# Two decode attention blocks, rewritten from heads in pairs to heads in fours, with one load queue and one V buffer

## The chip, the core and the metric

The kernel runs on one core of a Trainium2 chip. The core has five engines that run their own programs: TensorE (PE in the profile, its weight loads PEld), VectorE (DVE), ScalarE (ACT), GpSimd (POOL) and SyncE (SP), which here only issues transfers. Sixteen DMA engines move data between HBM and the on-chip memory SBUF; TensorE writes its results to PSUM. The metric is the device time of one execution in microseconds. Three runs of the kernel before took 678.93, 680.52 and 682.02 us, so the median is 680.52 us.

## What is computed

Two independent attention blocks, A and B, of the same sizes, each for one new token: D = 512, 32 heads of Dh = 128, a cache of Sk = 8192 keys and values, everything in bf16. The outputs of the two are put side by side, 1024 numbers.

```python
q = (x @ wq).reshape(B, Sq, H, Dh).transpose(0, 2, 1, 3)       # 1 x 32 x 1 x 128
scores = jnp.einsum("bhqd,bhkd->bhqk", q, k_cache) * (Dh ** -0.5)
p = softmax(scores, axis=-1)
o = jnp.einsum("bhqk,bhkd->bhqd", p, v_cache)
y = o.transpose(0, 2, 1, 3).reshape(B, Sq, H * Dh) @ wo        # 1 x 1 x 512
# out = concatenate([y of A, y of B], axis=-1)
```

Each head has 2 MB of keys and 2 MB of values, and each is read once: 64 heads are 268 MB. The four weight matrices (wq and wo of A and B) are 4 MB each. Little is computed per byte.

## The kernel before, in words

**Tiles.** Two heads form a step, so there are 32 steps: 16 of A, then 16 of B. The keys of a step fill one buffer: 64 partitions per head, and in each partition T = 128 consecutive keys of 128 numbers, which is one contiguous 32 KB row of HBM per partition, 4 MB per transfer. There are two such buffers for K (`kn`) and two for V (`vn`). A separate 4 MB buffer `wbuf` holds wq of A and later wo of A; wq of B sits at first in the second V buffer, and wo of B at the end in the first K buffer.

**A step.** Query rows are made on all partitions beforehand (`plan_q`, L263): `qbc[:, n, :]` holds, on each partition, the query of that partition's head. Then for step n:

- `plan_mul` (L287): VectorE multiplies the keys by the query in place, in four pieces of 128x4096;
- `plan_red` (L293): TensorE sums most of each product, 16 matmuls with the identity as weights that add up slices of 8 columns in PSUM (`rps`), for each half of the step; `plan_sr` (L306): VectorE sums the remaining 8 and writes the scores `s_sb`;
- `plan_max`, `plan_gmax`, `plan_exp` (L312 to L345): the maximum of each head is found over the partition's scores, then over partitions through a small TensorE transposition, and is spread over the partitions again by another small matmul; ScalarE forms the exponentials `pt` and their sums `rsum`;
- `plan_sum`, `plan_pv` (L347, L354): TensorE adds the sums over partitions and multiplies 128 times a V tile (as weights) by the two columns of `pt` for that tile, accumulating the outputs of both heads;
- `plan_o` (L364): VectorE scales by the reciprocal sum and writes `oD`, with the head's 128 numbers over the partitions.

`plan_pv` for step n-1 is placed in TensorE's program ahead of `plan_red` for step n.

**Order and queues.** `_Plan` (L24) records for each engine a list of instructions and waits on semaphores; every engine runs its list in order. K and all weights are loaded from SP's queue, V from ACT's queue. `load_k(n)` waits until the sums of step n-2 are through (its buffer), `load_v(n)` until the products of step n-2 are through; `load_v(1)` has to wait until wq of B has been used. TensorE's list is unrolled for the first three steps and from step 31 on; steps 3 to 30 are a loop of 14 rounds of two steps each (`_emit_loop`, L61), in which the waits compare semaphores with registers.

**The end.** `plan_relayout` (L385) turns `oD` into the layout in which wo lies in SBUF (`o2`). `plan_wo` (L400) multiplies 128 times a 128x128 piece of wo as weights by one column of `o2`, for A and then for B, after the last V has been used; then `plan_y` copies, `plan_out` transposes both results and one transfer writes them. wo of B is loaded in five pieces (16, 8, 4, 2 and 2 heads) behind wo of A, as rows of at least 2 KB.

Of the kernel before, what the change touches and what calls it, by code (L numbers as in the profile page):

```python
# [11 lines left out]
P = 128  # L12
# [11 lines left out]
class _Plan:  # L24
# [36 lines left out]
def _emit_loop(e, rounds):  # L61


    body = rounds[0]
    for r in rounds[1:]:
        assert len(r) == len(body)
        for (f0, c0, k0), (f1, c1, k1) in zip(body, r):
            assert (f0 is None) == (f1 is None) and c0 is c1
            assert f0 is None or k0 == k1
    grow = [rounds[1][i][2] - it[2] if it[0] is None else 0 for i, it in enumerate(body)]  # L70
    for n, r in enumerate(rounds):
        for it, d, base in zip(r, grow, body):
            assert it[0] is not None or it[2] == base[2] + n * d
    regs = {}
    for i, d in enumerate(grow):
        if d:
            regs[i] = e.alloc_register("w%d" % i)
            e.reg_mov(regs[i], body[i][2])
    with e.Fori(0, len(rounds)):
        due = []  # L80
        for i, it in enumerate(body):
            if i in regs:
                e.wait_ge(it[1].sem, regs[i])
                due.append(i)
                continue
            _emit(e, [it])
            if it[0] is not None:
                for j in due:
                    e.reg_add(regs[j], regs[j], grow[j])
                due = []  # L90
        for j in due:
            e.reg_add(regs[j], regs[j], grow[j])


def bass_concat_heads__mha_block_cached__gqa_block_cached__decode_kernel(
# [26 lines left out]
    HP = P // 2  # L122
    T = Sk // HP
    assert T == 128
    PA = H // 2
    NP = NA * PA
    NK = NV = 2
    CT = 32
    NCH = T // CT
    HT = T // 2  # L130
    DW = 512 // HT
    assert Dh % DW == 0

    WOG = [[(0, 32)], [(0, 16), (16, 8), (24, 4), (28, 2), (30, 2)]]
    RG = [32, 16, 8, 4, 2]

    with ExitStack() as st:
# [9 lines left out]
        wq_buf = [wbuf[:], vn[:, 1].rearrange("p t d -> p (t d)")]  # L147
        wq_sb = [b.rearrange("p (c n) -> p c n", c=C) for b in wq_buf]
        wo_sb = [b.rearrange("p (j n) -> p j n", n=NOUT)
                 for b in (wbuf[:], kn[:, 0].rearrange("p t d -> p (t d)"))]  # L150
        qbc = sb("qbc", [P, NP, Dh], BF16)
        pt = sb("pt", [P, 2, T, 2], BF16)
        s_sb = sb("s_sb", [P, 2, T], F32)
        xrow = sb("xrow", [1, NA, D], BF16)
        xb = sb("xb", [P, NA, C, P], BF16)
# [4 lines left out]
        hrow = sb("hrow", [1, 2, P], F32)  # L160
        m1 = sb("m1", [P, 2], F32)
        gm = sb("gm", [1, 2, 2], F32)
        negb = sb("negb", [P, NP], F32)
        rsum = sb("rsum", [P, 2, 2], F32)
        rinv = sb("rinv", [P, NP, 2], F32)
# [5 lines left out]
        NQ = NOUT // P  # L171
        yT = sb("yT", [P, NA, NQ], F32)
        out_q = sb("out_q", [NA * NQ, P], BF16)

# [4 lines left out]
        acc = ps("acc", [P, 2, 512])  # L179
# [3 lines left out]
        qyp = ps("qyp", [P, 512])  # L183
# [9 lines left out]
        s_wo = [[ctr("s_wo%d_%d" % (a, g)) for g in range(len(WOG[a]))] for a in range(NA)]  # L193
        s_k = [ctr("s_k%d" % i) for i in range(NK)]
        s_v = [ctr("s_v%d" % i) for i in range(NV)]
        s_out = ctr("s_out")
        c_pool, c_dve, c_act, c_pe = ctr("c_pool"), ctr("c_dve"), ctr("c_act"), ctr("c_pe")
        c_mul, c_red, c_sr, c_pv = ctr("c_mul"), ctr("c_red"), ctr("c_sr"), ctr("c_pv")
# [16 lines left out]
        i_h0 = const(lambda e: e.memset(hrow[:], 0.0))  # L215
        const(lambda e: e.memset(hrow[0:1, 0, 0:HP], 1.0), [i_h0])
        const(lambda e: e.memset(hrow[0:1, 1, HP:P], 1.0))
# [5 lines left out]
        k_in, v_in, wq_in, wo_in = {}, {}, {}, {}  # L223
        red_done, pv_done, q_done, wo_done = {}, {}, {}, {}

        def load_k(n):
            a, i = divmod(n, PA)
            src = ks[a][0, 2 * i:2 * i + 2].rearrange("h (p t) d -> (h p) (t d)", p=HP)
            k_in[n] = dma("SP", kn[:, n % NK].rearrange("p t d -> p (t d)"), src, s_k[n % NK],
                          [red_done.get(n - NK)])  # L230

        def load_v(n):
            a, i = divmod(n, PA)
            src = vs[a][0, 2 * i:2 * i + 2].rearrange("h (p t) d -> (h p) (t d)", p=HP)
            dst = vn[:, n % NV].rearrange("p t d -> p (t d)")
            need = {0: k_in[0], 1: q_done.get(1)}.get(n, pv_done.get(n - NV))
            v_in[n] = dma("ACT", dst, src, s_v[n % NV], [need])

        def load_wq(a):
            wq_in[a] = dma("SP", wq_buf[a], wqs[a].rearrange("(p c) n -> p (c n)", p=P), s_w[a])  # L240

        def load_wo(a, g):
            h0, n = WOG[a][g]
            src = wos[a][h0 * Dh:(h0 + n) * Dh, :].rearrange("(p j) n -> p (j n)", p=P)
            wo_in[a, g] = dma("SP", wo_sb[a][:, h0:h0 + n, :].rearrange("p j n -> p (j n)"), src, s_wo[a][g],
                              [q_done[0] if a == 0 else red_done[NP - 2]])


        for a in range(NA):
            def xmm(e, a=a):  # L250
                r = None
                for c in range(C):
                    r = e.matmul((misc if a == 0 else qyp)[:, c * P:(c + 1) * P],  # L253
                                 xrow[0:1, a, c:D:C], ones_bf[0:1, :], start=True, stop=True)
                return r
            m = op("PE", xmm, c_pe, [x_in, i_onesb])
            x_ready = op("ACT", lambda e, a=a: e.copy(
                xb[:, a].rearrange("p c m -> p (c m)"), (misc if a == 0 else qyp)[:]), c_act, [m])
        misc_free, qy_free = [x_ready], [x_ready]

        qbc_ready = {}

        def plan_q(a, j):  # L263

            def mm(e):
                r = None
                for hh in range(2):
                    for c in range(C):
                        w = wq_sb[a][:, c, 8 * j * Dh:8 * (j + 1) * Dh].rearrange(
                            "p (i h d) -> p i h d", h=2, d=Dh)[:, :, hh, :]  # L270
                        r = e.matmul(  # L271
                            qyp[hh * HP:(hh + 1) * HP, :].rearrange("p (i d) -> p i d", d=Dh),
                            xb[:, a, c, hh * HP:(hh + 1) * HP], w,
                            start=(c == 0), stop=(c == C - 1))
                return r
            m = op("PE", mm, c_pe, [x_ready, wq_in[a], qy_free[0]])
            q_done[a] = m
            n0 = a * PA + 4 * j
            qy_free[0] = op("ACT", lambda e: e.copy(
                qbc[:, n0:n0 + 4, :].rearrange("p i d -> p (i d)"), qyp[:]), c_act, [m])  # L280
            for n in range(n0, n0 + 4):
                qbc_ready[n] = qy_free[0]


        mul_done, sr_done, p_done, m_done, r_done, o_done = {}, {}, {}, {}, {}, {}

        def plan_mul(n, c):  # L287
            k = kn[:, n % NK, c * CT:(c + 1) * CT, :]
            mul_done[n, c] = op("DVE", lambda e: e.tensor_tensor(  # L289
                k, k, qbc[:, n:n + 1, :].broadcast_to([P, CT, Dh]), ALU.mult),  # L290
                c_mul, [k_in[n], qbc_ready[n]])

        def plan_red(n, h):  # L293

            def mm(e):
                r = None
                for i in range(Dh // DW):
                    r = e.matmul(  # L298
                        rps[:, h, :].rearrange("p (t d) -> p t d", d=DW), ident[:],
                        kn[:, n % NK, h * HT:(h + 1) * HT, i * DW:(i + 1) * DW],  # L300
                        start=(i == 0), stop=(i == Dh // DW - 1))
                return r
            last = (h + 1) * HT // CT - 1
            red_done[n] = op("PE", mm, c_red, [i_ident, mul_done[n, last], sr_done.get((n - 1, h))])

        def plan_sr(n, h):  # L306
            sr_done[n, h] = op("DVE", lambda e: e.tensor_reduce(  # L307
                s_sb[:, n % 2, h * HT:(h + 1) * HT],
                rps[:, h, :].rearrange("p (t d) -> p t d", d=DW), AX.X, ALU.add),
                c_sr, [red_done[n], p_done.get(n - 2)])  # L310
# [209 lines left out]
```

## Time and profile before

| what | value |
|---|---|
| median of three runs | 680.52 us |
| span of the profiled execution, first to last instruction | 678.1 us |
| time of the profiled execution beside its span | not listed; the median of the runs is 2.4 us above the span |
| read from HBM | 285.21 MB, 421 GB/s over the span |
| TensorE busy | 470.8 us (69%) |
| VectorE busy | 356.8 us (53%) |
| ScalarE busy | 43.9 us (6%) |
| mean granted TensorE clock | 0.737 of full speed |

The profile is of one execution. Its busy times are sums over the whole span; "idle before" says how long an engine had stood still before a group of instructions, and which event ended that. The view by stretches gives, for a window in microseconds from the start, the busy time of each engine (with the number of instructions), the granted TensorE clock, the mean busy share of the sixteen DMA engines and the rate at which they moved data. In short windows that share can read a little over 1.00.

### The profile page before, as it was taken

Reading aid. Unit: us, or ns where it says so; the run is one execution under the profiler, and the core shown is the slowest. Engines: PE = TensorE matmul, PEld = TensorE weight load, DVE = VectorE, ACT = ScalarE, POOL = GpSimd, SP = SyncE. Lnnn points to the kernel's source line nnn. Section 1 sums busy time; section 2 is a strip of 40 time slices with the busy share of each in tenths; the row PEclk is TensorE's granted clock in tenths of the full one; section 3 lists DMA queues with packets and bytes.
Section 4 is the critical chain, followed back from the end, with each engine's and each line's share of the span. In section 5 each row is a group of like instructions: output and inputs, shape, how many; then the busy total and the mean of one; then the engine's idle time right before and its main releaser. Section 6 shows DMA issues by size and latency. Waiting matters only on the chain.

```text
span 678.1 us, 12388 instructions
## 1 busy us (share of the span) xinstructions
PE 470.8 (69%) x5712; PEld 267.5 (39%) x5712; DVE 356.8 (53%) x345; ACT 43.9 (6%) x171; POOL 2.1 (0%) x13
## 2 busy tenths in 40 slices
PE   2662867787775677777767777776676877766686
PEld 1241433344443434444433344443433444434346
DVE  1505664455665555656655556566555565665540
ACT  1120000000000000000000000000000000000000
POOL 1000000000000000000000000000000000000000
PEclk9995778776667878765678787666878766678875
DMA  8999899999999999999999999999999999999994
GB/s 371 433 432 432 343 433 431 400 431 433 432 431 433 431 433 431 431 431 432 433 431 433 433 431 433 429 433 431 431 433 433 432 433 431 433 432 429 427 423 190
DMA packets 10403, 285.43 MB, mean 421 GB/s; under 512 B 1170, under 2 KB 1172, under 8 KB 1556
## 3 DMA queue, kind: packets, MB, share of 16 engines
q1 hardware_dynamic: 5776, 151.00, 52.1%
q10 hardware_dynamic: 4612, 134.22, 46.0%
q8 instruction: 10, 0.16, 0.1%
q14 instruction: 5, 0.04, 0.0%
HBM read 285.21 MB, written 0.00 MB: 421 GB/s over the span
## 4 chain that ended last, share of the span: by engine, by line
DMA 55%; PE 35%; DVE 5%; another core or an unknown queue 3%; issue 1%; ACT 1%; SPq 0%
DMA vn<-in_B_v_cache_dram 28%; DMA vn<-in_A_v_cache_dram 24%; PE rps L298 23%; PE acc L359 8%; DMA kn<-in_A_k_cache_dram 3%; DVE s_sb L307 2%; PE bmp L332 1%; DVE kn L289 1%; PE qyp L408 1%; PE mtp L319 1%; DVE m L313 1%; DVE gm L322 1%; ACT negb L336 0%; ACT pt L343 0%
## 5 line engine op out<-in xcount | busy, mean ns | idle before, releaser
L289 DVE TENSOR_TENSOR kn<-kn,qbc 128x4096 bf16<-128x4096 bf16 x128 | 286.7, 2283 | 104.5 <-DMA kn<-in_A_k_cache_dram 64.7
L298 PE MATMUL rps<-kn,ident 128*128 128x512 bf16 x1024 | 292.9, 457 | 16.4 <-DVE kn L289 16.4
L298 PEld LDWEIGHTS rps<-kn,ident 128*128 128x128 bf16 x1024 | 114.1, 114 | 180.8 <-issue 94.3
L359 PE MATMUL acc<-pt,vn 128*128 128x2 bf16 x4096 | 114.4, 165 | 81.8 <-DMA vn<-in_B_v_cache_dram 41.9
L359 PEld LDWEIGHTS acc<-pt,vn 128*128 128x128 bf16 x4096 | 112.1, 104 | 84.4 <-DMA vn<-in_B_v_cache_dram 43.3
L307 DVE TENSOR_REDUCE s_sb<-rps 128x64 f32<-128x512 f32 x64 | 44.3, 692 | 175.8 <-PE rps L298 175.8
L336 ACT ACTIVATE negb<-bmp 128x1 f32<-128x1 f32 x32 | 5.5, 171 | 592.3 <-PE bmp L332 592.3
L348 PE MATMUL misc<-rsum,ones_f 128*128 128x2 f32 x64 | 14.9, 302 | 39.3 <-ACT pt L343 39.0
L319 PE MATMUL mtp<-ident_f,m 128*1 128x128 f32 x64 | 12.1, 271 | 35.3 <-DVE m L313 35.3
L348 PEld LDWEIGHTS misc<-rsum,ones_f 128*128 128x128 f32 x64 | 12.2, 238 | 42.3 <-ACT pt L343 41.5
L343 ACT ACTIVATE pt<-s_sb,negb 64x128 bf16<-64x128 f32 x64 | 27.8, 435 | 1.8
L332 PE MATMUL bmp<-gm,hrow 1*128 1x1 f32 x128 | 19.3, 251 | 11.9 <-DVE gm L322 11.9
L332 PEld LDWEIGHTS bmp<-gm,hrow 1*128 1x128 f32 x128 | 16.6, 186 | 21.3 <-DVE gm L322 20.6
L319 PEld LDWEIGHTS mtp<-ident_f,m 128*1 128x1 f32 x64 | 2.7, 81 | 51.1 <-DVE m L313 51.1
L322 DVE TENSOR_REDUCE gm<-mtp 1x2 f32<-1x128 f32 x32 | 8.9, 278 | 15.1 <-PE mtp L319 15.1
L271 PE MATMUL qyp<-wbuf,xb 128*64 128x512 bf16 x32 | 7.7, 633 | 6.0 <-DMA wbuf<-in_A_wq_dram 3.9
L343 ACT ACTIVATION_READ_ACCUMULATOR pt<-s_sb,negb 64x1 f32 x64 | 11.6, 182 | 0.0
L313 DVE TENSOR_REDUCE m<-s_sb 128x1 f32<-128x128 f32 x32 | 9.2, 286 | 1.1
L366 DVE TENSOR_TENSOR oD<-acc,rinv 128x2 bf16<-128x2 f32 x32 | 4.9, 155 | 5.0 <-PE acc L359 5.0
L351 DVE RECIPROCAL rinv<-misc 128x2 f32<-128x2 f32 x32 | 5.3, 164 | 2.6 <-PE misc L348 2.6
L271 PEld LDWEIGHTS qyp<-wbuf,xb 128*64 128x64 bf16 x32 | 2.4, 158 | 10.7 <-issue 6.0
L253 PE MATMUL misc<-ones_bf,xrow 1*128 1x128 bf16 x4 | 0.6, 302 | 8.2 <-DMA xrow<-in_B_x_dram 8.2
(36 smaller groups left out, 40.2 us busy)
## 6 DMA issues: line engine op xcount, KB each, us to landing
kn<-in_A_k_cache_dram SPq DMA_DIRECT2D x16, 4096.0 KB, 23.5
vn<-in_A_v_cache_dram ACTq DMA_DIRECT2D x16, 4096.0 KB, 23.7
kn<-in_B_k_cache_dram SPq DMA_DIRECT2D x16, 4096.0 KB, 23.7
vn<-in_B_v_cache_dram ACTq DMA_DIRECT2D x16, 4096.0 KB, 23.5
wbuf<-in_A_wq_dram SPq DMA_DIRECT2D x1, 4096.0 KB, 12.2
vn<-in_B_wq_dram SPq DMA_DIRECT2D x1, 4096.0 KB, 36.8
wbuf<-in_A_wo_dram SPq DMA_DIRECT2D x1, 4096.0 KB, 42.9
kn<-in_B_wo_dram SPq DMA_DIRECT2D x1, 2048.0 KB, 29.6
```

The costliest lines, as they stand in the source:

```text
L271: r = e.matmul(qyp[hh * HP:(hh + 1) * HP, :].rearrange("p (i d) -> p i d", d=Dh), xb[:, a, c, hh * HP:(hh + 1) * HP], w, start=(c == 0), s ...
L289: mul_done[n, c] = op("DVE", lambda e: e.tensor_tensor(k, k, qbc[:, n:n + 1, :].broadcast_to([P, CT, Dh]), ALU.mult), c_mul, [k_in[n], qbc ...
L298: r = e.matmul(rps[:, h, :].rearrange("p (t d) -> p t d", d=DW), ident[:], kn[:, n % NK, h * HT:(h + 1) * HT, i * DW:(i + 1) * DW], start= ...
L307: sr_done[n, h] = op("DVE", lambda e: e.tensor_reduce(s_sb[:, n % 2, h * HT:(h + 1) * HT], rps[:, h, :].rearrange("p (t d) -> p t d", d=DW ...
L313: m_done[n] = op("DVE", lambda e: e.tensor_reduce(m1[:, n % 2:n % 2 + 1], s_sb[:, n % 2, :], AX.X, ALU.max), c_dve, [sr_done[n, 1]])
L319: m = op("PE", lambda e: e.matmul(mtp[0:1, 0:P], m1[:, n % 2:n % 2 + 1], ident_f[:], start=True, stop=True), c_pe, [m_done[n], i_identf, g ...
L322: gm_done[n] = op("DVE", lambda e: e.tensor_reduce(gm[:, n % 2, :], mtp[0:1, 0:P].rearrange("o (h p) -> o h p", h=2), AX.X, ALU.max), c_dv ...
L332: r = e.matmul(bmp[:, 0:1], hrow[0:1, h, :], gm[0:1, n % 2, h:h + 1], start=(h == 0), stop=(h == 1))
L343: p_done[n] = op("ACT", lambda e, h=h, q=q: e.activation(pt[q, n % 2, :, h], s_sb[q, n % 2, :], AF.Exp, bias=negb[q, n:n + 1], scale=scale ...
L348: m = op("PE", lambda e: e.matmul(misc[:, 0:2], ones_f[:], rsum[:, n % 2, :], start=True, stop=True), c_pe, [p_done[n], misc_free[0]])
L359: r = e.matmul(acc[:, n % 2, 0:2], vn[:, n % NV, t, :], pt[:, n % 2, t, :], start=(t == 0), stop=(t == T - 1))
L408: r = e.matmul(qyp[:, i:i + 1], wo_sb[a][:, j, i * P:(i + 1) * P], o2[:, a, j:j + 1], start=(j == 0 and i == 0), stop=(j == H - 1 and i == ...
```

## The change

**Tiles.** Four heads form a step, 32 partitions per head; there are 16 steps. A partition holds T = 256 keys, a contiguous 64 KB row of HBM, and a transfer of K or V is 8 MB. There are still two K buffers (now 64 KB per partition each) and only one V buffer of 64 KB. `wbuf` is gone: both wq lie in the V buffer before the first V, and both wo lie in the first K buffer after step 14.

**A step.** VectorE multiplies in four pieces of 128x8192, TensorE does four groups of 16 summing matmuls, with the two PSUM banks used in turn; one buffer each of scores, exponentials, maxima and outputs. The maximum is spread over 128 columns by a VectorE copy and then over the partitions by one matmul. ScalarE makes four exponentials (32 partitions by 256 each). The product with V is 256 matmuls of four columns.

**Queue and waits.** All transfers but the two small x rows and the output of A are issued by SP: wq of A, wq of B, K(0), K(1), V(0), K(2), V(1), K(3) and so on. V(n) waits until the product with V(n-1) is through, K(n+2) until the sums of step n are through.

**TensorE's program** is one loop of 17 rounds with the round number r in a register: groups 0 to 2 of the sums of step r (under a branch on r even or odd, which picks the K buffer), the product with V(r-1), group 3 of step r, the small matmuls for the maximum. In round 16 the work for wo of A and the first half of wo of B stands in the place of the sums. It has 1313 TensorE instructions with the weight loads counted, 1017 of them in the loop; before there were some 2690, with some 670 in the loop.

**The end.** After V(14) come wo of A and the first half of wo of B (16 heads), then V(15) in two parts (192 and 64 of the 256 keys of each partition), then the rest of wo of B in pieces of 8, 4, 2, 1 and 1 heads. The last three pieces are loaded with the head's rows over the partitions (rows of 1 KB), so that they are multiplied by `oD` directly and need no relayout. A is now 32 matmuls with the output column as weights and 512 columns of wo moving; its result is copied by ScalarE and written by ACT's queue before the end.

```diff
-    HP = P // 2
+    G = 4
+    HP = P // G
...
-    NK = NV = 2
-    CT = 32
...
+    NB = 4
+    HT = T // NB
...
+    VT = 192
...
+    WOB = [(0, 16, True), (16, 8, True), (24, 4, True), (28, 2, False), (30, 1, False), (31, 1, False)]
+    NPRE = 1
...
-        kn = sb("kn", [P, NK, T, Dh], BF16)
-        vn = sb("vn", [P, NV, T, Dh], BF16)
-        wbuf = sb("wbuf", [P, C * H * Dh], BF16)
...
+        kn = [sb("k%d" % i, [P, T, Dh], BF16) for i in range(2)]
+        vn = sb("vn", [P, T, Dh], BF16)
...
+        wq_buf = [vflat[:, a * WQ:(a + 1) * WQ] for a in range(NA)]
...
+        wo_buf = [kflat[0][:, a * H * NOUT:(a + 1) * H * NOUT] for a in range(NA)]
...
+            k_in[n] = dma("SP", kflat[n % 2], src, s_k[n % 2],
+                          [red_done(n - 2, NB - 1) if n >= 2 else None])
+
+        def load_v(n, need, t0=0, t1=T, c=None):
...
+            v_in[n] = dma("SP", vflat[:, t0 * Dh:t1 * Dh], src[:, t0 * Dh:t1 * Dh], c or s_v, [need])
...
+        load_k(0)
+        load_k(1)
+        for n in range(N):
+            if n < N - 1:
+                load_v(n, pv_done(n - 1) if n else q_done)
+                if n + 2 < N:
+                    load_k(n + 2)
+            plan_mul(n, 0)
+            plan_mul(n, 1)
+            if n >= 2:
+                plan_o(n - 2)
+            plan_sr(n, 0)
+            plan_mul(n, 2)
+            plan_sr(n, 1)
+            plan_mul(n, 3)
+            plan_sr(n, 2)
+            plan_sr(n, 3)
+            plan_max(n)
+            plan_exp(n)
+
+        woa_in = dma("SP", wo_buf[0], wos[0].rearrange("(p j) n -> p (j n)", p=P), s_woa,
+                     [red_done(N - 2, NB - 1)])
+        for g in range(NPRE):
+            load_wob(g)
+        load_v(N - 1, pv_done(N - 2), 0, VT)
+        load_v(N - 1, None, VT, T, s_v2)
+        for g in range(NPRE, len(WOB)):
+            load_wob(g)
...
+            with e.Fori(0, N + 1) as r:
+                with e.If(r < N):
+                    scores_of(r, range(0, NB - 1))
+                with e.If(r == N):
+                    _emit(e, prog[mid0:mid1])
+                with e.If(r > 0):
+                    w_o.wait()
+                    w_p.wait()
+                    e.matmul(misc[:, 0:G], ones_f[:], rsum[:], start=True, stop=True).then_inc(c_sum.sem, 1)
+                    w_v.wait()
+                    m = None
+                    for t in range(T):
+                        if t == VT:
+                            with e.If(r == N):
+                                e.wait_ge(s_v2.sem, 16)
+                        m = e.matmul(acc[:, 0:G], vn[:, t, :], pt[:, t, :],
+                                     start=(t == 0), stop=(t == T - 1))
+                    m.then_inc(c_pv.sem, 1)
...
+                with e.If(r < N):
+                    scores_of(r, range(NB - 1, NB))
+                    w_g.wait()
+                    e.matmul(mtp[0:1, 0:P], m1[:], ident_f[:], start=True, stop=True).then_inc(c_gx.sem, 1)
...
+            _emit(e, prog[mid1:])
```

More of the change, by code (lines that the diff above doesn't have):

```diff
@@ L58, in _emit, with __init__, wait, grow @@
             fn(e).then_inc(ctr.sem, k)
[L61 to L92, printed above, removed]
+class _Stepped:
+    def __init__(self, e, ctr, first, step):
+        assert first > 0 and step > 0
+        self.e, self.ctr, self.step = e, ctr, step
+        self.reg = e.alloc_register("w_" + ctr.name)
+        e.reg_mov(self.reg, first)
+    def wait(self):
+        self.e.wait_ge(self.ctr.sem, self.reg)
+    def grow(self):
+        self.e.reg_add(self.reg, self.reg, self.step)
 def bass_concat_heads__mha_block_cached__gqa_block_cached__decode_kernel(
@@ L232, in load_v @@
[L232 to L246, printed above, removed]
@@ L249, in bass_concat_heads__mha_block_cached__gqa_block_cached__decode_kernel @@
-        for a in range(NA):
[L250 to L282, printed above, removed]
@@ L285, in bass_concat_heads__mha_block_cached__gqa_block_cached__decode_kernel @@
[L285 to L290, printed above, removed]
-                c_mul, [k_in[n], qbc_ready[n]])
[L293 to L304, printed above, removed]
+            a, i = divmod(n, GA)
@@ new lines, in xmm @@
+        def xmm(e):
+            r = None
+            for a in range(NA):
+                for c in range(C):
+                    k = (a * C + c) * HP
+                    r = e.matmul(misc[:, k:k + HP], xrow[0:1, a, c:D:C], ones_bf[0:1, 0:HP],
+                                 start=True, stop=True)
+            return r
+        m = op("PE", xmm, c_pe, [x_in, i_pool])
+        x_ready = op("ACT", lambda e: e.copy(
+            xb[:].rearrange("p a c m -> p (a c m)"), misc[:, 0:NA * C * HP]), c_act, [m])
@@ new lines, in plan_max @@
+            op("DVE", lambda e: e.tensor_reduce(m1[:], s_sb[:], AX.X, ALU.max), c_g)
+            m = op("DVE", lambda e: e.tensor_reduce(
+                gm[:], mtp[0:1, 0:P].rearrange("o (h p) -> o h p", h=G), AX.X, ALU.max),
+                c_dve, [gx_done(n)])
+            op("DVE", lambda e: e.tensor_copy(
+                gmx[:].rearrange("o (h p) -> o h p", h=G),
+                gm[:].unsqueeze(2).broadcast_to([1, G, HP])), c_g, [m])
+        def plan_exp(n):
+            m = op("ACT", lambda e: e.activation(
+                negb[:, n:n + 1], bmp[:, 0:1], AF.Copy, scale=-scale), c_act, [bc_done(n)])
+            wait("ACT", m)
+            wait("ACT", pv_done(n - 1) if n else None)
@@ L354, in plan_pv @@
[L354 to L362 removed]
+                    pt[q, :, h], s_sb[q, :], AF.Exp, bias=negb[q, n:n + 1],
+                    scale=scale, accum_out=rsum[q, h:h + 1]), c_p)
@@ new lines, in bass_concat_heads__mha_block_cached__gqa_block_cached__decode_kernel @@
+        m = op("DVE", lambda e: e.tensor_copy(yT[:], yps[1][:, 0:NQ]), c_dve, [m])
+        m = op("PE", lambda e: e.matmul(bmp[0:NQ, 0:P], yT[:], ident[:], start=True, stop=True),
+               c_pe, [m, p_done[N - 1]])
+        m = op("DVE", lambda e: e.tensor_copy(out_b[:], bmp[0:NQ, 0:P]), c_dve, [m])
+        done_b = dma("SP", out[0][:, NOUT:2 * NOUT].rearrange("o (q n) -> (o q) n", q=NQ), out_b[:],
+                     s_out[1], [m])
+        wait("SP", done_a)
+        wait("SP", done_b)
```

350 lines of the change are left out of this document (177 added, 173 removed).

## The prediction

> **What bounds the kernel now.** I read the summary by slices first, then stretches of the span, then the chain that ended last. The slices show a transfer-bound kernel:
>
> ```profile
> span 678.1 us, 12388 instructions
> DMA  8999899999999999999999999999999999999994
> GB/s 371 433 432 432 343 433 431 400 431 433 432 431 433 431 433 431 431 431 432 433 431 433 433 431 433 429 433 431 431 433 433 432 433 431 433 432 429 427 423 190
> HBM read 285.21 MB, written 0.00 MB: 421 GB/s over the span
> DMA vn<-in_B_v_cache_dram 28%; DMA vn<-in_A_v_cache_dram 24%; PE rps L298 23%; PE acc L359 8%; DMA kn<-in_A_k_cache_dram 3%; DVE s_sb L307 2%; PE bmp L332 1%; DVE kn L289 1%; PE qyp L408 1%; PE mtp L319 1%; DVE m L313 1%; DVE gm L322 1%; ACT negb L336 0%; ACT pt L343 0%
> ```
>
> The DMA engines are nine tenths busy or more nearly everywhere, at 431 to 433 GB/s. The chain names TensorE work for a third of the span, but that is only how it passes from one V to the next: the slices say that data flow meanwhile. At 432 GB/s the 285.2 MB need 660.2 us, so 17.9 us of the span can be had by feeding the queue better. The stretches say where they lie (last columns: granted clock, DMA share, GB/s):
>
> ```profile
> 0.00:10.00 10.00, 1.04 (x8) 0.77 (x8) 2.29 (x10) 2.36 (x3) 2.05 (x13) 1.00 0.86 341
> 10.00:70.00 60.00, 32.76 (x253) 14.57 (x254) 20.57 (x15) 5.83 (x13) 0.00 (x0) 0.83 1.00 432
> 70.00:75.00 5.00, 3.53 (x19) 1.56 (x17) 1.77 (x4) 0.00 (x0) 0.00 (x0) 1.00 0.41 118
> 75.00:130.00 55.00, 41.32 (x496) 23.45 (x496) 31.17 (x27) 3.46 (x15) 0.00 (x0) 0.69 1.00 427
> 130.00:140.00 10.00, 7.22 (x145) 5.25 (x144) 7.78 (x7) 1.15 (x5) 0.00 (x0) 0.67 1.01 400
> 140.00:640.00 500.00, 357.98 (x4238) 202.38 (x4236) 280.00 (x262) 29.89 (x130) 0.00 (x0) 0.73 1.00 432
> 640.00:669.00 29.00, 20.37 (x349) 13.58 (x350) 12.57 (x20) 1.21 (x6) 0.00 (x0) 0.65 0.98 415
> 669.00:678.10 9.10, 6.54 (x217) 5.91 (x214) 0.60 (x3) 0.00 (x0) 0.00 (x0) 0.50 0.04 15
> ```
>
> Against 432 GB/s the losses are: the first 10 us 10 x (1 - 341/432) = 2.1; one hole at 70 to 75 us, 5 x (1 - 118/432) = 3.6; 75 to 130 us 0.6 and 130 to 140 us 0.7; 640 to 669 us 1.1; the last stretch, all but empty of transfers, 9.1 less its 0.3 of data. Together 17.1, and rounding of the rates covers the rest.
>
> **The change part by part.** *Bytes and the head of the queue.* The same bytes are read, and SP starts with wq of A as before: 0 for the first 10 us.
>
> *The hole at 70 us* came when both queues waited for buffers at the start. Now SP has wq A, wq B, K(0), K(1) without a compute wait, 25.2 MB: at the first stretch's loss and 432 GB/s they end at 60.4 us. V(0) needs only the queries, 64 matmuls beside the transfers (8 of the same width took 1.93 us, row at 13.12 us below: 15.4 us), so it is queued long before. K(2) needs the sums of step 0, K(0) landing (41 us) plus some 30: 71, while V(0) runs until 80. The hole goes: 3.6 gained. The smaller shortfalls (0.6, 0.7, 1.1) go the same way: 2.5 gained.
>
> *The steady rounds.* A round moves 16.78 MB: 38.8 us at 432. Does compute keep under it with one V buffer? The durations:
>
> ```profile
> L289 DVE TENSOR_TENSOR kn<-kn,qbc 128x4096 bf16<-128x4096 bf16 x128 | 286.7, 2283 | 104.5 <-DMA kn<-in_A_k_cache_dram 64.7
> L307 DVE TENSOR_REDUCE s_sb<-rps 128x64 f32<-128x512 f32 x64 | 44.3, 692 | 175.8 <-PE rps L298 175.8
> L343 ACT ACTIVATE pt<-s_sb,negb 64x128 bf16<-64x128 f32 x64 | 27.8, 435 | 1.8
> L343 ACT ACTIVATION_READ_ACCUMULATOR pt<-s_sb,negb 64x1 f32 x64 | 11.6, 182 | 0.0
> 643.60 3.57 PE L359 MATMUL acc<-pt,vn 128*128 128x2 bf16 x128 [2.02 <-DMA vn<-in_B_v_cache_dram]
> 647.03 6.16 PE L298 MATMUL rps<-kn,ident 128*128 128x512 bf16 x16
> 653.06 3.61 PE L298 MATMUL rps<-kn,ident 128*128 128x512 bf16 x16
> 657.78 0.38 PE L319 MATMUL mtp<-ident_f,m 128*1 128x128 f32 x2 [1.11 <-DVE m L313]
> ```
>
> A multiplication of twice the size is 2 x 2.283 = 4.57 us (four: 18.3, as before for as many keys). A group of 16 sums is 3.61 us or, when the clock is low, 6.16. The product with V is 256 matmuls, 2 x 3.57 = 7.1; its four columns in place of two I price at nothing, since 28 ns each is far more than two columns' share of a 512-column matmul at 226 ns. With K(n) landed at 0 and fast groups: products 0 and 1 end at 4.6 and 9.1, the output's two small VectorE steps 9.5, sum 0 (0.69) 10.1, product 2 14.7, sum 1 15.4, product 3 20.0; TensorE's group 2 ends at 18.3; V(n-1) lands at 19.4; product with V 19.9 to 27.0; group 3 30.6, its sum 31.3, maximum, transposition, maximum and copy 1.5 more: VectorE is free at 32.8. With all four groups at 6.16: group 2 ends at 23.1, the product with V at 30.7, VectorE is free at 39.3. So V(n) is issued 27 to 31 us into the round, 8 to 12 us before K(n+1) ends at 38.8, and K(n+2) at 31 to 37, over 20 us before V(n) ends. Of the moved waits: behind SP's wait for the product with V stands only K(n+2), which isn't due yet. ScalarE's four exponentials (0.43 us for 128 wide and 0.18 each before; at most twice that, 4.9 us together) end by 39 in the fast case and have until V(n) lands at 58. One V buffer costs 0, covered by the 8 us; without cover each microsecond late costs one per round. The mean granted clock is 0.73 of full, nearer to the fast row's stretch than to all groups at 6.16; I take 33 to 36.
>
> *Row size and one queue.* The steady rate is for two queues and 32 KB rows. One queue alone stood here:
>
> ```profile
> 13.12 1.93 PE L271 MATMUL qyp<-wbuf,xb 128*64 128x512 bf16 x8 [3.90 <-DMA wbuf<-in_A_wq_dram]
> 22.72 8.90 DVE L289 TENSOR_TENSOR kn<-kn,qbc 128x4096 bf16<-128x4096 bf16 x4 [18.94 <-DMA kn<-in_A_k_cache_dram]
> ```
>
> wq of A and K(0) landed 9.60 us apart, with no V issued yet: 4.19 MB, 437 GB/s. From 427 (the 55 us stretch) to 437 that is +7.6 to -7.6 us over 660. I take 432, where 500 us stand: 0.
>
> *V(15) and the end.* While the product with V(14) runs (until 7.6 to 11.3 us after V(14) lands), wo of A and half of B move, 6.29 MB, 14.6 us: no hole. wo of A's 32 matmuls (at 0.21 to 0.43 us, 7 to 14) run beside the 14.6 us of V(15)'s first part. Behind V(15) 2.1 MB of wo are left, 4.9 us; the last 64 products (1.8) and the scaling fit in it. So the last piece of wo ends the transfers. Before, this came after them:
>
> ```profile
> 668.01 3.31 PE L408 MATMUL qyp<-o,wbuf 128*128 128x1 bf16 x118 [1.58 <-issue]
> 671.66 3.63 PE L408 MATMUL qyp<-o,kn 128*128 128x1 bf16 x128 [0.35 <-DVE yT L415]
> 675.33 0.16 DVE L415 COPY yT<-qyp 128x4 f32<-128x4 f32 x1 [3.81 <-PE qyp L408]
> 675.55 0.59 PE L419 MATMUL bmp<-ident_f,yT 128*8 128x128 f32 x2 [0.25 <-DVE yT L415]
> 676.18 0.28 DVE L422 CAST out_q<-bmp 8x128 bf16<-8x128 f32 x1 [0.69 <-PE bmp L419]
> 676.49 0.37 SPq L201 DMA_DIRECT2D out_dram<-out_q  x1
> ```
>
> 246 matmuls go off the path; what stays is 4 matmuls (0.1), copy, transposition, copy, write, 678.1 - 675.3 = 2.8, and 0.4 from the last byte to TensorE's start (an estimate; the write's issue to the end of the span, 1.6, is a whole small transfer, so it lies between 0 and 1.6): 3.3 in place of 9.1, 5.8 gained.
>
> *Small pieces.* 0.52 MB now come in 1 KB rows, 1.2 us at 432. No such rows stand in the trace. Extra cost from 0 to 1.2 us (half rate); the nearest row is the end of before, which with pieces down to 2 KB lost 1.1: I take 1.1.
>
> Sum: 3.6 + 2.5 + 5.8 - 1.1 = 10.8, so a span of 667.3. What lies around a span is not listed; the median stands 2.4 above it, and with that 669.7 us.
>
> **The rivals.**
> 1. *The matmul clock makes compute the bound* (slower). The point is VectorE free at 38.8; each microsecond over costs 15, and the gain is gone at 39.5. All groups as the 6.16 row give 39.3, + 7.5 us, 677. At 0.43 us for every matmul, the rate at which the 6.16 us group starts (its weight loads, below), a group is 6.8 and the round 42: + 48, 718 us. For it: the round leaves TensorE idle some 8 us before the next product, and the clock was 0.65 to 0.73. Against: a group of 3.61 follows right behind the slow one.
>
> ```profile
> 647.41 0.15 PEld L298 LDWEIGHTS rps<-kn,ident 128*128 128x128 bf16 x1 [0.28 <-issue]
> 647.84 0.15 PEld L298 LDWEIGHTS rps<-kn,ident 128*128 128x128 bf16 x1 [0.28 <-issue]
> ```
> 2. *64 KB rows read worse* (slower). The sixteen streams now start twice as far apart in HBM. The gain is gone at a rate 1.6% lower; at 3% it is 20 us, 690 us. No row speaks for it but the 427 stretch. The Trainium skill, "DMA: Bandwidth & Descriptors", "Latency and other measured facts", lists falling copy rates for partition pitches that are large powers of two, 207 of 214 GB/s at 512 KiB, down to half at megabytes; by that ratio, an estimate, the time would also be about 690. No run here shows it, and the pitch is 64 KB.
> 3. *Taken branches stall TensorE's program* (slower). The loop is longer than before's and jumps several times per round. Price of a fetch behind a full queue: the 1 KB x rows, issued at 0.8, landed at 8.18. One such 7.4 us stall between V and group 3 lifts the fast round to 40.2: + 21, 691 us.
>
> ```profile
> 8.18 0.61 PE L253 MATMUL misc<-ones_bf,xrow 1*128 1x128 bf16 x4 [8.18 <-DMA xrow<-in_B_x_dram]
> 387.09 0.59 PE L348 MATMUL misc<-rsum,ones_f 128*128 128x2 f32 x2 [1.30 <-ACT pt L343]
> 405.35 0.38 PE L348 MATMUL misc<-rsum,ones_f 128*128 128x2 f32 x2 [1.30 <-ACT pt L343]
> q8 instruction: 10, 0.16, 0.1%
> ```
>
>    Against: before's loop goes back every second step, and both neighbours of these two waits are alike, 1.30 us ended by ScalarE; and 0.16 MB is TensorE's whole program once, so no round fetched again. The Trainium skill, "Runtime: NRT & Kernel Launch", "Instruction fetch mechanics", says that a jump out of a window of two pages forces a fetch; before's loop of some 670 instructions is longer than two of its 256-instruction pages, and by the rows the rule doesn't hold for TensorE.
> 4. *The end saves little* (faster by less): the 1 KB pieces run at a sixth of the rate, 7.3 us in place of 1.2, of which 1.1 is counted: + 5, 674.7 us. For it: the slices' rate falls in the last stretch that had small pieces (415). Against: that stretch lost only 1.1 in all.
>
> **How the numbers follow.** The forecast 0.72, with 664 to 674 of its own (rate and small pieces); rival 1 0.08, rival 2 0.07, rival 3 0.05, rival 4 0.08. Forecast, rival 4 and the mild form of rival 1 hold 8 in 10: 663.5 to 679. A measurement tells 0.5%, 3.4 us, from no change: faster (under 677.1) 0.81, same 0.05, slower 0.14.
>
> **What would show it.** Right: DMA share 1.00 without a hole from 10 us to within 4 us of the end; V(n) issued some 10 us before K(n+1) lands; VectorE waiting for K each round; the last thing before the final copy a wait for wo's last piece. Wrong: holes at each V (rival 1 or 3, told apart by granted clock against idle "issue" time on TensorE), or a full share at under 425 GB/s (rival 2).

## The result and the profile after

The changed kernel takes 672.16 us (median of four runs, 671.92 to 672.37); the kernel before took 679.94 us in the runs beside it. The ratio is 0.9886, with a 95% interval of 0.9864 to 0.9909: faster by 7.8 us, where 10.8 were forecast. The profiled execution has a span of 670.2 us.

The summary by slices of the changed kernel, the queues, and the costliest groups:

```profile
span 670.2 us, 11845 instructions
PEclk9659797979777676978776697877658796676886
DMA  9999999999999999999999999999999999999996
GB/s 376 438 438 429 435 391 375 438 438 439 438 434 438 434 426 396 438 438 438 438 438 438 438 438 438 430 438 430 426 411 430 438 438 434 438 438 438 406 448 278
q1 hardware_dynamic: 6184, 285.22, 98.7%
q8 instruction: 5, 0.08, 0.1%
L307 DVE TENSOR_TENSOR k<-k,qbc 128x8192 bf16<-128x8192 bf16 x64 | 281.4, 4418 | 94.7 <-DMA k<-in_A_k_cache_dram 57.0
L461 PE MATMUL rps<-k,ident 128*128 128x512 bf16 x1024 | 296.2, 458 | 171.0 <-DVE k L307 163.3
L490 PE MATMUL acc<-pt,vn 128*128 128x4 bf16 x4096 | 108.9, 165 | 6.1 <-DMA vn<-in_B_v_cache_dram 3.8
```

The kernel is bound by its transfers as before. The hole of before at 70 to 75 us is gone, and the end without transfers is short. But slices 6 and 7 (84 to 117 us) show less than the others, and there is the hole that the forecast did not have (stretches; granted clock, DMA share, GB/s last):

```profile
90.00:98.00 8.00, 6.71 (x142) 4.92 (x143) 6.76 (x4) 0.00 (x0) 0.00 (x0) 1.00 0.95 410
98.00:102.00 4.00, 3.88 (x140) 3.67 (x137) 0.00 (x0) 0.00 (x0) 0.00 (x0) 0.62 0.15 66
102.00:110.00 8.00, 6.09 (x20) 2.19 (x18) 2.09 (x5) 0.01 (x1) 0.00 (x0) 0.76 0.99 393
```

For some 4 us next to nothing moves. The programs of SP and of TensorE say why:

```profile
73.35 0.33 SPq L205 DMA_DIRECT2D k<-in_A_k_cache_dram  x1
101.66 0.33 SPq L205 DMA_DIRECT2D vn<-in_A_v_cache_dram  x1
107.36 0.33 SPq L205 DMA_DIRECT2D k<-in_A_k_cache_dram  x1
```

```profile
57.53 3.63 PE L461 MATMUL rps<-k,ident 128*128 128x512 bf16 x16 [1.66 <-DVE k L307]
67.86 5.47 PE L461 MATMUL rps<-k,ident 128*128 128x512 bf16 x16 [6.70 <-issue]
94.89 6.74 PE L490 MATMUL acc<-pt,vn 128*128 128x4 bf16 x256
101.75 2.72 PE L461 MATMUL rps<-k,ident 128*128 128x512 bf16 x6
```

K(2), issued at 73.35, is the last load in the queue; V(1) comes only at 101.66, when the product with V(0) is through, and by then the queue has run dry. Behind that stands group 3 of step 0, which TensorE starts only at 67.86, after 6.70 us in which it waits for nothing that the profile shows (the bracket names `issue`). The same place in the next round costs 0.1 us (product with V to 101.6, group 3 at 101.75).

After this the rounds are as forecast. VectorE's first two multiplications of some steps; where a bracket stands, it had waited for K:

```profile
109.44 8.74 DVE L307 TENSOR_TENSOR k<-k,qbc 128x8192 bf16<-128x8192 bf16 x2
143.47 8.74 DVE L307 TENSOR_TENSOR k<-k,qbc 128x8192 bf16<-128x8192 bf16 x2
182.25 8.76 DVE L307 TENSOR_TENSOR k<-k,qbc 128x8192 bf16<-128x8192 bf16 x2 [4.52 <-DMA k<-in_A_k_cache_dram]
298.37 8.76 DVE L307 TENSOR_TENSOR k<-k,qbc 128x8192 bf16<-128x8192 bf16 x2 [4.62 <-DMA k<-in_A_k_cache_dram]
337.06 8.76 DVE L307 TENSOR_TENSOR k<-k,qbc 128x8192 bf16<-128x8192 bf16 x2 [5.14 <-DMA k<-in_B_k_cache_dram]
```

A round that doesn't wait takes 34.0 us (109.44 to 143.47), one that does 38.69 (298.37 to 337.06), 433.6 GB/s for its 16.78 MB. The end:

```profile
657.43 6.97 PE L490 MATMUL acc<-pt,vn 128*128 128x4 bf16 x256 [1.36 <-DMA vn<-in_B_v_cache_dram]
664.82 1.01 PE L419 MATMUL yps<-o,k 128*128 128x1 bf16 x32 [0.42 <-DMA k<-in_B_wo_dram]
666.88 0.82 PE L419 MATMUL yps<-oD,k 128*128 128x1 bf16 x16 [0.18 <-DMA k<-in_B_wo_dram]
667.73 0.16 DVE L435 CAST yT<-yps 128x4 bf16<-128x4 f32 x1 [3.13 <-PE yps L419]
668.56 0.35 SPq L205 DMA_DIRECT2D out_dram<-out_b  x1
```

The last pieces of wo are waited for one after the other. From the first matmuls of wo behind the last V (664.82) to the end of the span are 5.4 us; before, from 668.01, they were 10.1.

### The profile page after: what moved, and what is told of

Same layout as the page of the kernel before. It is cut to its first block, busy times and chain, and to the rows that moved or that the text cites. A ratio compares the mean times of both kernels' runs of the same rounds, so it can differ in the third digit from the quotient of the medians.

```text
span 670.2 us, 11845 instructions
## 1 busy us (share of the span) xinstructions
PE 439.5 (66%) x5453; PEld 241.9 (36%) x5453; DVE 342.6 (51%) x229; ACT 62.2 (9%) x151; POOL 2.0 (0%) x10
## 4 chain that ended last, share of the span: by engine, by line
DMA 60%; PE 27%; DVE 11%; issue 1%; SPq 0%
DMA vn<-in_B_v_cache_dram 19%; PE rps L461 15%; DMA k<-in_B_k_cache_dram 14%; DMA k<-in_A_k_cache_dram 13%; PE acc L490 12%; DVE k L307 10%; DMA vn<-in_A_v_cache_dram 9%; DMA k<-in_B_wo_dram 4%; DVE s_sb L312 1%; SPq L205 0%; DVE m L319 0%; PE mtp L499 0%; DVE gm L320 0%; PE misc L483 0%; DVE gmx L323 0%
## 5 line engine op out<-in xcount | busy, mean ns | idle before, releaser
L461 PE MATMUL rps<-k,ident 128*128 128x512 bf16 x1024 | 296.2, 458 | 171.0 <-DVE k L307 163.3
L307 DVE TENSOR_TENSOR k<-k,qbc 128x8192 bf16<-128x8192 bf16 x64 | 281.4, 4418 | 94.7 <-DMA k<-in_A_k_cache_dram 57.0
L461 PEld LDWEIGHTS rps<-k,ident 128*128 128x128 bf16 x1024 | 112.5, 114 | 342.8 <-DVE k L307 173.3
L490 PE MATMUL acc<-pt,vn 128*128 128x4 bf16 x4096 | 108.9, 165 | 6.1 <-DMA vn<-in_B_v_cache_dram 3.8
L335 ACT ACTIVATE pt<-s_sb,negb 32x256 bf16<-32x256 f32 x64 | 54.8, 856 | 1.9
L335 ACT ACTIVATION_READ_ACCUMULATOR pt<-s_sb,negb 32x1 f32 x64 | 15.9, 248 | 0.0
L277 PE MATMUL yps<-vn,xb 128*32 128x512 bf16 x64 | 7.3, 630 | 10.6 <-DMA vn<-in_B_wq_dram 6.0
L502 PE MATMUL bmp<-ones_f,gmx 1*128 1x1 f32 x32 | 6.2, 259 | 9.9 <-DVE gmx L323 9.9
L405 PE MATMUL yps<-k,o 128*1 128x512 bf16 x32 | 8.4, 429 | 0.0
L341 DVE RECIPROCAL rinv<-misc 128x4 f32<-128x4 f32 x16 | 2.8, 174 | 10.1 <-PE misc L483 10.1
L319 DVE TENSOR_REDUCE m<-s_sb 128x1 f32<-128x256 f32 x16 | 6.7, 420 | 0.5
```

The lines of the kernel that those rows point to most:

```text
L277: r = e.matmul(yps[j % 2][hh * HP:(hh + 1) * HP, :].rearrange("p (i d) -> p i d", d=Dh), xb[:, a, c, :], w, start=(c == 0), stop=(c == C - 1))
L307: mul_done[n, h] = op("DVE", lambda e: e.tensor_tensor(k, k, qbc[:, n:n + 1, :].broadcast_to([P, HT, Dh]), ALU.mult), c_mul, [k_in[n], qbc ...
L319: op("DVE", lambda e: e.tensor_reduce(m1[:], s_sb[:], AX.X, ALU.max), c_g)
L335: p_done[n] = op("ACT", lambda e, h=h, q=q: e.activation(pt[q, :, h], s_sb[q, :], AF.Exp, bias=negb[q, n:n + 1], scale=scale, accum_out=rs ...
L405: r = e.matmul(yps[0][0:1, :], o2[:, 0, j:j + 1], wo_sb[0][:, j, :], start=(j == 0), stop=(j == H - 1))
L461: r = e.matmul(rps[:, h % 2, :].rearrange("p (t d) -> p t d", d=DW), ident[:], kn[slot][:, h * HT:(h + 1) * HT, i * DW:(i + 1) * DW], star ...
```

## The experiments

All times are medians; 672.16 us is the changed kernel's. The runs are from several chips; the kernel before took 678.5 to 679.4 us beside them. The question was first what makes the hole, which costs 4.8 us (K(4) landed at 182.25; at 38.69 us a round from K(0) at 42.02, with seven loads or 3.5 rounds between the two, it would have been 177.4), then what in the change gives the gain.

**1. Round 0 in a straight line.** The program of TensorE's first round is written out ahead of the loop, so that it does not jump over the code of the product with V.

```diff
-            with e.Fori(0, N + 1) as r:
...
+            scores(0, range(0, NB - 1))
+            scores(0, range(NB - 1, NB))
+            gmax()
+            with e.Fori(1, N + 1) as r:
```

> Round 0 of TensorE's program stands in a straight line ahead of the loop, so that no jump over the product with V comes before group 3 of step 0; nothing else is changed. Theory (the 6.70 us of 'issue' idle time ahead of group 3 in round 0 is a wait for code that the jump skipped to; it makes the whole first half late by some 7 us, V(1) is issued after K(2) has landed, and the transfers stand still from 98 to 102 us): the idle time falls under 1 us, V(1) is issued at about 95 us in place of 101.7, the hole goes, K(4) lands about 4.7 us earlier, span about 665.5, time about 667.4. Rival (compute alone is too slow to have V(1) issued in time, the stall only adds to it): the hole stays at 2 us or more and the time at 669.5 to 672.2.

670.26 us. The wait ahead of group 3 of step 0 is gone, K(2) is issued at 66.21 in place of 73.35. But other waits appear inside the first product with V:

```profile
62.55 3.63 PE L461 MATMUL rps<-k,ident 128*128 128x512 bf16 x16 [1.31 <-DVE k L307]
87.93 3.16 PE L500 MATMUL acc<-pt,vn 128*128 128x4 bf16 x120
92.48 3.55 PE L500 MATMUL acc<-pt,vn 128*128 128x4 bf16 x127 [1.38 <-issue]
99.65 0.40 PE L500 MATMUL acc<-pt,vn 128*128 128x4 bf16 x9 [3.63 <-issue]
```

The product stops after 120 and after 247 matmuls, so V(1) is issued at 100.08, only 1.6 us earlier, and 1.9 us are gained. My number (95 us, 667.4) was missed: the wait moved. That it moved to the next code that runs for the first time speaks for the theory, but did not settle it. The queue of instructions, `q8`, does more: in the changed kernel two of its five packets of 16 KB are moved while TensorE stands still ahead of group 3 (they end at 64.62 and 65.24 us, and it goes on at 67.86). Here one packet ends at 90.87, ahead of the start again at 92.48, and one at 98.32, ahead of that at 99.65.

**2. The straight line, and group 3 of step 0 three times.** The lines are against those of run 1.

```diff
-            scores(0, range(NB - 1, NB))
+            scores(0, range(NB - 1, NB), 3)
```

> As the straight-line version, but group 3 of step 0 is done three times (32 summing matmuls more, some 7.3 us, once). Theory (only the lateness counts, not its cause): V(1) is issued at about 101 to 102 us, a hole of about 4 us without any transfer is back, and the time is within 1 us of the changed kernel's 672.2. Rival (the time that the straight line saves comes from elsewhere, the loop's branches in all rounds): the time stays within 1 us of the straight-line version.

674.27 us; V(1) is issued at 104.61 and the stretch from 100 to 105 us moves 7 GB/s. V(1) is later than forecast, since waits inside the first product with V are there too (2.1 and 0.3 us), and the time is 2.1 us above the changed kernel where 1 was forecast. But the direction holds, and the rival is out: 7 us of work more in step 0, with all later rounds unaltered, cost 4.0 us.

**3. One round more, dry.** In a first round of the loop only the product with V is done, on wq and on exponentials that are zero, while TensorE has nothing else to do; the first real product overwrites its result. V(0) then waits for this product.

```diff
-            with e.Fori(0, N + 1) as r:
+            with e.Fori(0, N + 2) as r:
...
-                with e.If(r > 0):
+                with e.If(r != 1):
                     w_o.wait()
```

> The changed kernel with one round more at the beginning of TensorE's loop, in which only the product with V is done, on whatever lies in the V buffer (wq) and on exponentials that are zero, while TensorE waits for K(0) anyway; its result is overwritten. So the loop's code has been run through once before step 0. Theory (the 6.70 us ahead of group 3 in step 0, and in the straight-line version the 1.4 and 3.6 us inside the first product with V, are waits for code that is needed for the first time): these waits fall in the time before K(0) lands at 42 us, there is none of over 1 us after it, V(1) is issued at about 95 us, no hole at 98 to 102 us, time 668 us. Rival (the wait belongs to step 0, its semaphores or its branch, whatever ran before): some 6 us of idle 'issue' time ahead of group 3 of step 0 stay, and the time is 672.2.

668.31 us, against 672.15 for the changed kernel in the same set of runs. The waits now stand in the dry round:

```profile
32.21 0.56 PE L486 MATMUL misc<-rsum,ones_f 128*128 128x4 f32 x2 [5.67 <-issue]
32.63 1.85 PE L493 MATMUL acc<-pt,vn 128*128 128x4 bf16 x64
39.10 3.58 PE L493 MATMUL acc<-pt,vn 128*128 128x4 bf16 x128 [4.62 <-issue]
46.53 1.87 PE L493 MATMUL acc<-pt,vn 128*128 128x4 bf16 x64 [3.85 <-issue]
49.83 9.49 PE L463 MATMUL rps<-k,ident 128*128 128x512 bf16 x32 [1.43 <-issue]
91.39 6.72 PE L493 MATMUL acc<-pt,vn 128*128 128x4 bf16 x256
```

5.67 us at the jump, then 4.62 and 3.85 us, the latter two 128 matmuls apart, which with their weight loads are 256 instructions. In the first real product the same code runs through in 6.72 us. Each of the three waits ends 1.6 to 1.9 us after a packet of instructions (these end at 30.54, 37.51 and 44.67), and from 60 to 600 us this queue moves nothing. So these are waits for code that runs for the first time. The dry round lasted longer than I thought, so the first sums start some 3 us late (49.83), V(0) is issued at 48.43 and V(1) at 98.14, just in time. The Trainium skill, "Runtime: NRT & Kernel Launch", "Instruction fetch mechanics", says that an engine's code arrives in blocks of 256 instructions and that a jump to code outside the blocks at hand waits for a transfer; the distance of 128 matmuls and the wait at the jump agree. The Trainium skill says in the same place that the cost of crossing into the next block is mostly hidden; here, beside a full queue of loads, it was hidden for some blocks (no wait follows the packet that ends at 52.32 us in the changed kernel) and not for others (3.63 us in run 1).

**4. The changed kernel again**, beside that run.

> The changed kernel unaltered, beside the one with the extra round on the same chip, for their difference: 672.2 us, within 0.5.

672.15 us, so the difference of 3.8 us to the dry round is of the same runs.

**5. K(0) ahead of wq of B.** On top of the straight line (1), compute starts 10 us earlier.

```diff
+        wq_in = [load_wq(0)]
+        load_k(0)
+        wq_in.append(load_wq(1))
...
+            scores(0, range(0, 2))
+            _emit(e, prog[qa:mid0])
+            scores(0, range(2, NB))
+            gmax()
```

> The straight-line version with K(0) loaded ahead of wq of B, and the queries of B made between groups 1 and 2 of step 0, so that compute starts some 10 us earlier; the loop and its waits for code stay. Theory (the time hangs on whether V(1) is issued before K(2) has landed, at some 100 us): V(1) is issued at 95 us or earlier in spite of waits for code, no hole before 140 us, time 668 us, 2 us under the straight-line version. Rival (a hole moves to another place of the start, V(0) being issued later): no faster than the straight-line version's 670.3.

668.00 us (667.90 to 668.10), ratio to the kernel before 0.9851 (0.9817 to 0.9885): the fastest version here. A wait for code of 3.11 us is still inside the first product with V, but V(1) is issued at 92.53, and from the second step on every K lands 38.7 us after the one before. The three cures and the aggravation order themselves by one number:

| kernel | V(1) issued at, us | time, us |
|---|---|---|
| K(0) first | 92.53 | 668.00 |
| dry round | 98.14 | 668.31 |
| straight line | 100.08 | 670.26 |
| changed kernel | 101.66 | 672.16 |
| straight line, group 3 three times | 104.61 | 674.27 |

Up to some 98 us, when K(2) is through, V(1)'s issue costs next to nothing (0.3 us between the first two rows, which differ in more than that); from 98.14 to 104.61, 6.5 us of lateness cost 6.0.

**6. One queue alone.** The kernel before, with V on SP's queue too.

```diff
-            v_in[n] = dma("ACT", dst, src, s_v[n % NV], [need])
+            v_in[n] = dma("SP", dst, src, s_v[n % NV], [need])
```

> The kernel before with V loaded from SP's queue as well; one part of the change done alone. Theory (row length makes the higher rate): K keeps landing every 19.42 us, 680 us but for what the start does. Rival (one queue makes it): every 19.35 us, and 2.4 us faster, 677.5. A new wait is possible at the start, where V(2) then stands ahead of K(4) in one queue; the interval between landings in the later steps is what tells.

674.13 us, ratio to the kernel before 0.9927 (0.9900 to 0.9954), which neither theory had. The interval of the later steps (145.34, 203.49, 261.65 and 319.81 us mark every third step) is 19.39 us, 38.77 for two, between the theories. The rest lies at the start and the end, by stretches of this kernel:

```profile
60.00:100.00 40.00, 28.27 (x340) 15.96 (x339) 21.87 (x20) 2.31 (x10) 0.00 (x0) 0.76 1.00 428
640.00:664.00 24.00, 18.23 (x347) 12.54 (x345) 8.08 (x16) 1.15 (x5) 0.00 (x0) 0.71 0.98 412
664.00:671.50 7.50, 3.91 (x121) 3.33 (x120) 0.44 (x2) 0.00 (x0) 0.00 (x0) 0.50 0.11 40
```

From 60 to 100 us it moves 428 GB/s where the kernel before moved 390, which is 40 x 38 / 432 = 3.5 us: the hole at 70 us does not form. At the end the loads land in the order of their need: the last product with V starts at 653.34 in place of 661.83, and the matmuls of wo run as wo lands, with 7 us in place of 9 behind the last transfer. One changed word gives two thirds of what the whole rewrite gives (5.2 of 7.8 us).

**7. 32 KB rows on one queue.** The changed kernel with each load in two transfers of half the row.

```diff
+            for h0 in (0, T // 2):
+                s = slice(h0 * Dh, (h0 + T // 2) * Dh)
+                k_in[n] = dma("SP", kflat[n % 2][:, s], src[:, s], s_k[n % 2],
...
```

> The changed kernel with each load of K and V cut into two transfers of 4 MB, 32 KB of each 64 KB row, on the same queue; one size is changed. In the changed kernel K lands every 38.69 us in most rounds, before it was 2 x 19.42 = 38.85. Theory (longer rows make the difference): 38.85 us, 2.4 us slower over 15 rounds, 674.6. Rival (one queue in place of two makes it): 38.69 us, 672.2.

673.64 us; K lands every 38.85 us (183.07, 221.92, 260.78, 299.65). With 64 KB rows it is 38.69, so the longer transfer gives 0.16 us a round, as the first theory had it; the time is 1.5 us longer, where 2.4 were forecast. Rows and the size of a transfer were halved together; which of them counts stays open. Nor is the length of the rows the whole of it: run 6, with 32 KB rows and one queue, had 38.77.

**8. wo of B ahead of V(15).**

```diff
-        for g in range(NPRE):
+        for g in range(len(WOB)):
             load_wob(g)
         load_v(N - 1, pv_done(N - 2), 0, VT)
         load_v(N - 1, None, VT, T, s_v2)
-        for g in range(NPRE, len(WOB)):
-            load_wob(g)
```

> The changed kernel with all of wo of B loaded ahead of V(15), so that V(15)'s second part is the last transfer; undoes the part of the change that puts pieces of wo behind the last V. Theory (behind the last byte then stand the last 64 products with V, 1.8 us, the scaling and 64 matmuls of wo, 1.8 us, in place of four matmuls): 3 to 4 us slower than the changed kernel, 675 to 676 us. Rival (the end is set by something else, the landing of the last transfer whatever it is): within 1 us of 672.2.

675.72 us, 3.6 slower, as the theory has it: the last product with V runs from 662.50 to 669.5 and the matmuls of wo come behind it. The pieces behind the last V are worth their place.

**9. Group 3 twice, and four times, in every round.**

```diff
-                    for i in range(Dh // DW):
+                    for i in (list(range(Dh // DW)) * (2 if h == NB - 1 else 1)):
```

> The changed kernel with group 3 of the sums done twice in every step: 16 matmuls more per round, 3.6 us, behind the product with V. Theory (VectorE stands idle 4.0 to 5.3 us before each K, and V is issued some 11 us early, so compute has that much room): no change, 672.2 within 2 us (the first round, which is late already, gets 3.6 us later and can widen the one hole by that). Rival (one V buffer leaves no room, any added work shows in every round): + 3.6 us times 15, about 725 us.

> The changed kernel with group 3 of the sums done four times in every step, 10.9 us more of TensorE work per round. With it done twice VectorE's wait for K had all but gone (a round that isn't waiting for K took 37.5 us), so the room is used up. Theory (compute and transfers are two chains of 34 and 38.7 us per round; the longer one sets the time): a round takes 37.5 + 7.2 = 44.7 us, VectorE never waits for K after the first, time about 672 + 15 x 6 = 762 us. Rival (one more buffer's worth of room is hidden somewhere): under 700 us.

Twice: 675.00 us, 2.8 more (0.8 beyond the 2 us that were forecast), not 54. A round without a wait takes 37.5 us (116.75 to 154.24), still under 38.7; the loss fits the start, where V(1) is issued at 105.46. Four times: 779.37 us (one run); VectorE's rounds follow each other every 44.4 us and never wait for K after the first. The forecast of 762 left out two things. The end gets longer by 8 us (69.2 in place of 61.3 from the start of step 15). And from K(0) to K(15) lie 15 rounds of compute, but only 14.5 of transfers, since K(1) follows K(0) without a V between them. So compute and transfers are two chains, the longer one sets the time, and the changed kernel has 4.7 us of room per round.

## Why the prediction was right or wrong

The time, 672.16, lies in the range, 2.5 us above the 669.7 forecast; the direction and the mechanism (fewer gaps in a transfer-bound kernel) held. One sign of being right failed, though: the transfers do not run from 10 us on without a hole.

- **The hole at 70 us.** It went, but "the hole goes: 3.6 gained" failed as a step. I followed the start only as far as K(2) and stopped one load short. At the start two K lie ahead of V(0), so K(1) lands 19 us after K(0), while a round of compute takes 34: compute is behind from the start, and V(1), which needs the product with V(0), is due when K(2) ends. That alone would have been in time, as the dry round shows; the 6.70 us for new code made it late. The cost is 4.8 us at K(4)'s landing. So "one V buffer costs 0, covered by the 8 us" failed here too: at the start there was no such cover, and with one buffer V(1) cannot be issued before the product with V(0) is through.
- **Rival 3, stalls at branches.** I gave it 0.05 and priced a stall at 7.4 us from the landing of the x rows; it was 6.70. Its place was wrong: I looked at every round and found, rightly, that before's loop isn't fetched again. In the changed kernel too the later rounds run without such a wait, and the queue of instructions shows 5 packets, 0.08 MB, in all. What I didn't ask is when its code comes in for the first time. So my reading that the rule of the Trainium skill ("Runtime: NRT & Kernel Launch", "Instruction fetch mechanics") doesn't hold for TensorE fits the later rounds and is wrong for the first pass, in which a jump did wait for code.
- **The steady rounds.** Right: VectorE free at 33 to 36, measured 34.0, so rival 1 is out; V(n) issued 27 to 31 us into the round, measured a little less, 26.2 (298.37 to 324.57); one V buffer costs nothing in these rounds, as run 9 shows by its room.
- **Rate.** 432 GB/s was taken, 433.6 came in most rounds, inside the stated bounds: 2.1 us better over 14.5 rounds, of which slower rounds, above all one of 39.69 us, took back 1.1. Rival 2 is out: the falling copy rates that the Trainium skill ("DMA: Bandwidth & Descriptors", "Latency and other measured facts") lists for partition pitches of 512 KiB and more do not show at this pitch of 64 KB.
- **V(15).** Right, no hole: V(14) had landed at 628.2, V(15) was issued at 635.1, and wo ahead of it ran until about 642.7.
- **The end and the small pieces.** 61.3 us from the landing of K(15) (608.92) to the end of the span. At 433.6 GB/s the loads behind K(15) need 58.0, so the last should land at 667.0; it landed at 667.4. So the 1 KB pieces cost at most 0.4 and not 1.1, and rival 4 is out. Behind this landing 2.8 us remained, with the last four matmuls, where 2.9 were forecast. The last data move until about 666.9 us (172 GB/s from 665 to 666, then 22 GB/s with a DMA share of 0.06, nothing from 667 on), so some 0.5 us lie between them and TensorE's start and 3.3 to the end of the span, as forecast.
- **The sum.** The steps of the forecast (K(0) at 41, 14.5 rounds of 38.84, then 58.3 for the loads behind K(15), 1.1 and 3.3) add up to 666.8, half a microsecond under its sum of 667.3. Against them K(0) was 1.0 later; from K(0) to K(15) it took 566.9 in place of 563.1, which is the hole's 4.8 less 1.0 for the rounds; the end was 61.3 in place of 62.7. Together that is 3.4 more, the 670.2 measured. What lies around the span was 1.7 in the profiled execution, not 2.4. So that the time is off by only 2.5 us is in part luck: the hole and the late K(0), 5.8 us, were partly offset by what came out better.
- **What gives the gain.** I read the gain off single gaps and did not see that one part of the change, the single queue, removes the hole at the start and a good part of the end by itself (run 6).

## What to carry to other kernels

In a transfer-bound kernel with deep buffers, follow the queue load by load until the pattern repeats, with the compute time of the first rounds beside it: the start has another order than the steady state, and one late issue is never made good. Code counts as a load of its own: the first pass through a long loop waits behind the bulk transfers, so let it happen while the engine has nothing to do, or start compute earlier. And put loads into one queue in the order of their need before thinking of larger tiles.

## What the runs showed of the hardware that I had not expected

- New code made TensorE wait beside a full queue of loads: 5.7 to 6.8 us at a jump over code, 0.3 to 4.6 us within straight code, where the waits lie 128 matmuls apart. The 16 KB packets with the code took 0.9 to 2.1 us each. In the kernel before, and in it with one queue, the waits without a visible cause were 0.8 to 2.1 us. The longer rows are not the reason for the long wait at the jump: with the 32 KB rows of run 7 it was 6.02 us, and in the changed kernel 6.70 and, in run 4, 6.15.
- On one queue the changed kernel moved 433.6 GB/s with 8 MB loads of 64 KB rows and 431.9 with 4 MB loads of 32 KB rows (38.69 and 38.85 us a round). The kernel before, with 32 KB rows on one queue, came to 432.7.
- The DMA engines do not end together: from 666 to 666.9 us the last pieces moved at a share of 0.06, which is one engine of sixteen.
- One round of the profiled execution took 39.69 us in place of 38.69 (K landing at 453.17 and 492.86), and the same round of run 7 39.88 (455.06 and 494.94); in run 5 all are alike. This isn't explained.
